# Moving row tiles in one transfer over 128 partitions, in a fused convolution and feed-forward kernel

## The chip, the cores and the metric

The kernel runs on one core of one Trainium2 chip. The metric is the device time of one execution in microseconds. A core has TensorE (PE, matrix products), VectorE (DVE), ScalarE (ACT), GpSimd (POOL) and SyncE (SP). Transfers between memory (HBM) and the on-chip SBUF, whose tiles have up to 128 partitions, are issued from the queues of SP, ACT and POOL and carried out by 16 DMA engines.

## What is computed

All arrays are float32, S = 2048 rows of D = 576 columns. `A_q` is `x`; the hidden width of the feed-forward part is 4608.

```python
xn = layernorm(x)                                  # x = A_q, over the columns
# A: short causal convolution of k (4 taps, per column), times v,
kv = causal_conv4(k, shift_k) * v
# then a causal convolution over all 2048 rows by FFT, per column
y = irfft(rfft(pad(kv)) * rfft(pad(ssm_k)))[:S] + kv * ssm_D
# B: feed-forward
ffn = relu(xn @ w1) @ w2                           # w1 576 x 4608, w2 4608 x 576
out = x + xn * y + ffn
```

## The kernel before

**Rows.** The 2048 rows are split as row = 32p + 16u + t, with p in 0..63, u in 0..1 and t in 0..15. Tile t holds 128 rows of 576 columns: partitions 0 to 63 are the 64 rows of u = 0, partitions 64 to 127 those of u = 1. In memory the 64 rows of one u lie 32 rows apart, and the two series lie 16 rows from each other. The views `x`, `k`, `v`, `out` have the shape (u, p, t, d). `halves(u)` gives the partitions of one half, and `move` loads or stores a tile, or a pair of tiles t and t + 1, in two transfers, one for each half. Its argument `queues` names the queue of each.

**The feed-forward part** sets most of TensorE's work. It takes the hidden units in 36 visits over 18 pairs of 256 (`NPAIR`), in two halves of the rows; each block has four tiles (512 rows). A product in float32 is made of three products of operands that are rounded into a high and a low part (`split_into`, `relu`). `load_w1(n)` loads the first weights of a visit: 4 x 128 rows in one transfer, and the remaining 64 rows (576 = 4 x 128 + 64) twice, once into partitions 0 to 63 and once into 64 to 127. `load_w2` loads the second weights into `r`; `split_w2` turns them into `w`, which the `pso` matmuls read. `mm1` makes the `psh` matmuls.

**The row tiles of x** come in pairs: `load_acc` into the `acc` tiles, where the sums are kept as well, `later_xT` into `rows` for the second half, and `load_rest` into `xt` for the last step. Finished sums of the first eight tiles go to memory as `fin` and come back as `ft`.

**The convolution** is a stream (`conv`) whose steps are inserted between the matmuls of the feed-forward part by a count of work (`tick`). It has four parts: the transform of the filter (`fk`, tiles `zk`), that of kv (`fx`: `load` fetches a tile of k and one of v two tiles ahead of their use, results go to `zx`), the products and second transforms (`fm`, results to `zy`), and the way back (`fo`: loads `zo`, `xt`, and `ft`; stores eight tiles of the output from `y` on POOL's queue). The other eight tiles of the output are stored from `acc` at the very end; the very last tile goes in column halves, each in two transfers, one on SP's queue and one on ACT's.

**Order.** The program is written in the order of the feed-forward visits; a scheduler then orders each engine's instructions. Each engine and each queue takes its instructions strictly in that order.

Of the kernel before, what the change touches and what calls it, by code (L numbers as in the profile page):

```python
# [17 lines left out]
P = 128  # L18
# [13 lines left out]
BT = T // NB  # L32
# [5 lines left out]
U = S // (T * A1)  # L38
# [71 lines left out]
def h3_ffn_kernel(ctx: ExitStack, tc, x, k, v, shift_k, ssm_k, ssm_D, w1, w2, fwd, inv, mid, out):  # L110
    nc = tc.nc
    x = x[0].rearrange("(p u t) d -> u p t d", u=U, t=T)
    k = k[0].rearrange("(p u t) d -> u p t d", u=U, t=T)
    v = v[0].rearrange("(p u t) d -> u p t d", u=U, t=T)
    out = out[0].rearrange("(p u t) d -> u p t d", u=U, t=T)
# [31 lines left out]
    acc = {}  # L147

    def place(b):

        return 1 - b if b < HB else b - HB

    def halves(u):

        return slice(u * A1, (u + 1) * A1), slice((1 - u) * A1, (2 - u) * A1)

    def move(tile_, rows, t, store=False, queues=(nc.sync, nc.sync)):
        for u in range(U):
            a, b = tile_[halves(u)[0]], rows[u, :, t]
            queues[u].dma_start(*((b, a) if store else (a, b)))  # L160

    pairs = {}

    def load_x(t, tag, bufs, late=False, **queues):
        pair = xp.tile([P, 2, D], F32, tag=tag, name=f"acc{t}", bufs=bufs)
        if late:
            with here():
                nc.vector.memset(pair[:, :, :1], 0.0)
        move(pair, x, slice(t, t + 2), **queues)
        return pair  # L170

    def load_acc(t, **queues):
        pairs[t] = load_x(t, f"acc{place(t // BT)}", BT // 2, **queues)
        acc[t], acc[t + 1] = pairs[t][:, 0, :], pairs[t][:, 1, :]

    def stats(t, src):
# [26 lines left out]
    done = {}  # L203
# [100 lines left out]
    def later_xT(b):  # L304
# [16 lines left out]
        for i in range(0, BT, 2):  # L321
            with here():
                if b == HB:
                    nc.vector.memset(hold[:, i * D:i * D + 1], 0.0)
                move(hold[:, i * D:(i + 2) * D].rearrange("p (t d) -> p t d", t=2), x,
                     slice(b * BT + i, b * BT + i + 2))
# [110 lines left out]
    def load_w1(n):  # L437
        f0 = (n % NPAIR) * FC
        r1 = both_w1[:, 5:] if n < NPAIR and n % 2 else both_w1
        for o, step in ((0, P), (P, FC - P)) if n == 0 else ((0, FC),):  # L440
            f, to = slice(f0 + o, f0 + o + step), slice(o, o + step)
            queue = nc.gpsimd if n == 0 and o == 0 else nc.sync
            queue.dma_start(r1[:, :4, to], w1[:4 * P, f].rearrange("(c p) f -> p c f", p=P))
            for h in range(2):
                queue.dma_start(r1[64 * h:64 * h + 64, 4, to], w1[4 * P:, f])
        raw_w[n] = r1
        weights[n] = {}

# [166 lines left out]
    def unit(ns, s, b, i, h, last):  # L615

        t = b * BT + i
        cols = slice(i * P, (i + 1) * P)
        final = b >= HB and last
        if final:  # L620
            while t not in added:
                next(stream)
        ps = ps_o.tile([P, 512], F32, tag="o", name=f"pso{ns[0]}_{t}_{h}")
        dc = slice(h * NH, (h + 1) * NH)
        seq = []
        for n in ns:
            for j in range(FT):
                hh, ll = hid[n, s, j]
                w = weights[n]["w2", h][:, :, j]
                seq += [(hh[:, cols], w[:, 0]), (hh[:, cols], w[:, 1]), (ll[:, cols], w[:, 0])]  # L630
        for c, (a, m) in enumerate(seq):
            done["pe"] = nc.tensor.matmul(ps[:, :NH], a, m, start=c == 0,  # L632
                                          stop=c == len(seq) - 1)
            if c % 6 == 5:
                tick(6 * NH)
        if b == 0:
            done["acc"] = nc.vector.scalar_tensor_tensor(
                acc[t][:, dc], ps[:, :NH], rstd[:, t:t + 1], acc[t][:, dc],
                op0=OP.mult, op1=OP.add)
        else:  # L640
            done["acc"] = nc.vector.tensor_tensor(acc[t][:, dc], ps[:, :NH], acc[t][:, dc],  # L641
                                                  OP.add)
        if final and t == T - 1:
            for u, queue in ((0, nc.sync), (1, nc.scalar)):
                queue.dma_start(out[u, :, t, dc], acc[t][halves(u)[0], dc])
        elif last and h:
            if t < HT:
                if t % 2:
                    nc.sync.dma_start(fin[t // 2], pairs[t - 1])
            elif t == T - 2:  # L650
                move(acc[t], out, t, store=True)
            elif t % 2:
                move(pairs[t - 1], out, slice(t - 1, t + 1), store=True)
# [7 lines left out]
    def fill():  # L661
        room = 2
        while work and work[0][0] <= room:
            size, args = work.pop(0)
            unit(*args)
            room -= size
# [23 lines left out]
    @contextmanager  # L690
    def here():


        with tc.issue_after(done["acc"].ins), tc.issue_after(done["act"].ins):
            yield

    def conv():
# [5 lines left out]
        with hold_pool as kp:  # L703
# [3 lines left out]
            win, gates, sums, uses = {}, {}, {}, [0]  # L707

            def slot(i):
                return both[:, i * D:(i + 1) * D]  # L710
# [7 lines left out]
            def load(t):  # L718
                win[t] = slot(WIN + t % (KS + 1))
                if t >= 0:  # L720
                    move(win[t], k, t, queues=(nc.sync, nc.sync))
                    gates[t] = slot(GATE + t % 2)
                    move(gates[t], v, t, queues=(nc.sync, nc.sync))
                else:
                    nc.gpsimd.memset(win[t][0:1, :], 0.0)
                    nc.sync.dma_start(win[t][1:A1, :], k[1, 0:A1 - 1, T + t, :])
                    nc.sync.dma_start(win[t][A1:, :], k[0, :, T + t, :])

            def first_loads():
                with here():  # L730
                    for j, t in enumerate((0, *range(-1, -KS, -1), 1)):
                        if j < KS:
                            nc.sync.dma_start(sk[:, j, :], shift_k[j:j + 1, :].to_broadcast([P, D]))
                        load(t)

            with tc.tile_pool(name="fk", bufs=2) as fp:
# [3 lines left out]
                for b in range(0, NH // Q, KB):  # L740
                    with here():
                        nc.vector.memset(kr[:, b:b + KB, :1], 0.0)
                    for q in range(4):
                        h, r = divmod(q, 2)
# [35 lines left out]
                for n, t2 in enumerate(order):  # L780
                    stk, nxt = nxt, []
                    u, t = divmod(t2, T)
# [94 lines left out]
        with tc.tile_pool(name="fm", bufs=2) as fp:  # L877
# [22 lines left out]
            def run(hi, lo, d, h):  # L900
# [7 lines left out]
                return ps[:, :NH], cols  # L908

            load(zk, 0, "k")  # L910
            load(zx, 0, "x")
            yield -PAUSE
# [69 lines left out]
        with tc.tile_pool(name="fo", bufs=2) as fp:  # L982
# [37 lines left out]
            def add(i):  # L1020
                if i >= 0:
                    t = order[i]
                    to, more = (ys[i], sums[i]) if t < HT else (acc[t], acc[t])
                    with here():
                        nc.vector.scalar_tensor_tensor(to, ys[i], rstd[:, t:t + 1], more,
                                                       op0=OP.mult, op1=OP.add)
                    if t < HT:
                        move(to, out, t, store=True, queues=(nc.gpsimd, nc.gpsimd))
                    else:
                        added.add(t)  # L1030

# [5 lines left out]
            for n, (t, u) in enumerate(units):  # L1037
# [7 lines left out]
                for h in range(2):  # L1045
# [20 lines left out]
                    yield W_FO  # L1066
            gate(T - 1)
            add(T - 1)


# [9 lines left out]
    def tick(cost):  # L1080

        if clock["done"] or clock["ffn"] < clock["until"]:
            clock["ffn"] += cost
            return
        clock["ffn"] += cost
        clock["conv"] += rate * cost
        if clock["conv"] < 0:
            return
        try:
            c = next(stream)  # L1090
        except StopIteration:
            clock["done"] = True
            return
        if c < 0:
            clock["conv"] = min(clock["conv"], 0.0)
            clock["until"] = clock["ffn"] - c
        else:
            clock["conv"] -= c

    warm = xp.tile([P, 512], mybir.dt.bfloat16, tag="m5", name="warm", bufs=1)  # L1100
    nc.vector.memset(warm, 0.0)
    for t in range(0, BT, 2):
        load_acc(t, queues=(nc.sync, nc.scalar))
    load_w1(0)
    table = const.tile([P, 1], F32, name="table")
    nc.vector.memset(table, 1.0)
# [12 lines left out]
    with tc.issue_after(done["act"].ins):  # L1119
        split_rest(0, 1)  # L1120
    load_w1(1)
    for t in range(BT, HT, 2):
        load_acc(t)
# [57 lines left out]
    for q, (n, s) in enumerate(visits):  # L1181
        half, m = divmod(n, NPAIR)
        b = HB + s if half else 1 - s
# [70 lines left out]
```

## Time and profile before

| | |
|---|---|
| median of 3 runs | 1058.05 us (1057.59 to 1059.14) |
| profiled execution | 1057.93 us, of which the span of the instructions is 1056.2 us |
| granted TensorE clock | 1.0 |
| busy: PE, DVE, ACT, POOL | 1047.1, 743.9, 550.7, 398.2 us |
| moved by DMA | 204.45 MB, mean 194 GB/s |

The profile is one execution. An engine's busy time counts its instructions of work; transfers are issued by instructions of a queue (SPq, ACTq, POOLq) and carried out by the DMA engines, whose share is a mean over all 16. The chain of waits goes back from the last instruction: at each step to what released it.

### The profile page before, as it was taken

How to read it: one execution, taken by the hardware profiler on the slowest of the kernel's cores; microseconds unless marked ns; L12 is line 12 of the kernel's file. 1: busy time of each engine (PE TensorE's matmuls, PEld its weight loads, DVE VectorE, ACT ScalarE, POOL GpSimd, SP SyncE). 2: the span in 40 equal slices, each digit the busy share in tenths (PEclk: the TensorE clock that was granted, in tenths of full speed). 3: DMA queues.
4: the chain of work that ended last, by engine and by line, in shares of the span. 5: the costliest groups of instructions: out<-in, count | busy, mean ns of one | idle time of the engine just before them, and what ended most of it. 6: DMA issues, size and time to landing. Idle time of an engine off the chain costs nothing.

```text
span 1056.2 us, 20042 instructions
## 1 busy us (share of the span) xinstructions
PE 1047.1 (99%) x7153; PEld 988.2 (94%) x7153; DVE 743.9 (70%) x1316; ACT 550.7 (52%) x1201; POOL 398.2 (38%) x398
## 2 busy tenths in 40 slices
PE   8999999999999999999999999999999999999998
PEld 5889999999999999999999999999999999999997
DVE  5539778787776788773477887778877773666664
ACT  5226566534343444433277787687777773444341
POOL 4133333333222333352443534343433444544641
PEclk9999999999999999999999999999999999999999
DMA  9944867777566766755876655656555648776864
GB/s 230 205 98 134 226 172 209 201 227 212 151 191 178 212 177 197 239 164 187 277 219 193 192 173 166 195 172 197 167 177 175 183 127 264 221 228 214 287 191 113
DMA packets 156304, 204.45 MB, mean 194 GB/s; under 512 B 32846, under 2 KB 122704, under 8 KB 155181
## 3 DMA queue, kind: packets, MB, share of 16 engines
q1 hardware_dynamic: 143308, 189.00, 60.5%
q0 software_dynamic: 12576, 13.44, 5.6%
q8 instruction: 56, 0.92, 0.4%
q10 hardware_dynamic: 320, 0.74, 0.3%
q14 instruction: 44, 0.35, 0.1%
HBM read 133.92 MB, written 55.05 MB: 179 GB/s over the span
## 4 chain that ended last, share of the span: by engine, by line
PE 97%; DVE 1%; DMA 1%; ACT 0%; issue 0%; SPq 0%; DVEq 0%
PE pso L632 43%; PE psh L569 22%; PE psb L545 14%; PE psf L907 7%; PE psa L545 6%; PE psf L687 3%; PE psf L1051 1%; PE psf L1053 1%; DMA acc<-in_x 1%; DVE bn L179 0%; PE psf L278 0%; ACT hh L551 0%; DVE lok L897 0%; DVE acc L641 0%; DVE yl L932 0%
## 5 line engine op out<-in xcount | busy, mean ns | idle before, releaser
L632 PE MATMUL pso<-w,hh 128*128 128x288 f32 x2304 | 468.9, 295 | 1.6 <-ACT w L531 0.8
L632 PEld LDWEIGHTS pso<-w,hh 128*128 128x128 f32 x2304 | 372.5, 188 | 9.8 <-ACT w L531 1.2
L632 PE MATMUL pso<-w,ll 128*128 128x288 f32 x1152 | 329.5, 295 | 0.0
L431 POOL TENSOR_TENSOR g<-both_w,g 128x256 fp32r<-128x256 f32 (+2 forms) x145 | 168.4, 1167 | 374.1 <-ACT g L469 322.4
L569 PE MATMUL psh<-b,g 128*128 128x512 f32 x864 | 218.2, 395 | 0.5 <-ACT b L226 0.2
L632 PEld LDWEIGHTS pso<-w,ll 128*128 128x128 f32 x1152 | 213.3, 188 | 1.1
L569 PEld LDWEIGHTS psh<-b,g 128*128 128x128 f32 x864 | 156.9, 188 | 30.5 <-DVE b L227 0.5
L641 DVE TENSOR_TENSOR acc<-pso,acc 128x288 f32<-128x288 f32 x232 | 101.7, 450 | 61.9 <-PE pso L632 59.1
L431 POOL TENSOR_TENSOR w<-r,w 128x576 fp32r<-128x576 f32 x72 | 113.0, 1570 | 53.8 <-ACT w L531 53.7
L551 ACT ACTIVATE hh<-psh 128x512 fp32r<-128x512 f32 x72 | 42.9, 597 | 143.8 <-PE psh L569 143.8
L552 DVE SCALAR_TENSOR_TENSOR ll<-psh,hh 128x512 fp32r<-128x512 f32 x72 | 49.4, 687 | 69.8 <-ACT hh L551 69.3
L545 PE MATMUL psb<-t,g 128*128 128x256 f32 x648 | 94.9, 280 | 0.1
L545 PEld LDWEIGHTS psb<-t,g 128*128 128x128 f32 x648 | 85.5, 188 | 0.4 <-DVE psa L600 0.3
L469 ACT ACTIVATE g<-both_w 128x256 fp32r<-128x256 f32 (+2 forms) x145 | 76.3, 543 | 9.9 <-PE psb L545 6.6
L498 POOL TENSOR_TENSOR both_w<-both_w 128x256 f32<-128x256 f32 x72 | 62.8, 891 | 30.3 <-DMA both_w<-in_w 29.0
L545 PE MATMUL psa<-b,g 128*128 128x256 f32 x432 | 63.1, 280 | 0.0
L551 ACT ACTIVATE hh<-psa 128x512 fp32r<-128x512 f32 x36 | 21.5, 598 | 72.9 <-PE psa L545 72.7
L545 PE MATMUL psb<-b,g 128*128 128x256 f32 x432 | 57.5, 281 | 0.0
L545 PEld LDWEIGHTS psa<-b,g 128*128 128x128 f32 x432 | 56.6, 188 | 0.0
L545 PEld LDWEIGHTS psb<-b,g 128*128 128x128 f32 x432 | 54.4, 188 | 0.2
L950 DVE TENSOR_TENSOR k<-psf,k 128x288 f32<-128x288 f32 x64 | 29.0, 454 | 35.1 <-ACT sw L949 33.3
L673 POOL DMA_DIRECT2D wx<-in_fwd x32 | 17.6, 551 | 95.3 <-PE psf L687 85.6
(135 smaller groups left out, 1695.3 us busy)
## 6 DMA issues: line engine op xcount, KB each, us to landing
r<-in_w SPq DMA_DIRECT2D x72, 288.0 KB, 4.0
zy<-vo SPq DMA_DIRECT2D x64, 288.0 KB, 2.9
zo<-zy SPq DMA_DIRECT2D x32, 576.0 KB, 4.4
both_w<-in_w SPq DMA_DIRECT2D x35, 512.0 KB, 4.2
zk<-zk SPq DMA_DIRECT2D x64, 144.0 KB, 2.6
ztk<-zk SPq DMA_DIRECT2D x32, 288.0 KB, 3.4
ztx<-zx SPq DMA_DIRECT2D x32, 288.0 KB, 3.5
k<-k SPq DMA_DIRECT2D x64, 144.0 KB, 3.3
```

Of the source, the lines that this page charges most:

```text
L431: return nc.gpsimd.tensor_tensor(dst, src, hi, OP.subtract)
L469: nc.scalar.activation(hi, src, AF.Copy)
L498: nc.gpsimd.tensor_tensor(dst, a, b, op)
L545: done["pe"] = nc.tensor.matmul(ps, a, m, start=start and i == 0, stop=i == len(seq) - 1, skip_group_check=not start)
L551: done["act"] = nc.scalar.activation(hh, ps, AF.Relu)
L552: lows.append(nc.vector.scalar_tensor_tensor(ll, ps, 0.0, hh, op0=OP.max, op1=OP.subtract))
L569: done["pe"] = nc.tensor.matmul(ps, a, m, start=i == 0, stop=i == len(seq) - 1)
L632: done["pe"] = nc.tensor.matmul(ps[:, :NH], a, m, start=c == 0, stop=c == len(seq) - 1)
L641: done["acc"] = nc.vector.tensor_tensor(acc[t][:, dc], ps[:, :NH], acc[t][:, dc], OP.add)
L687: nc.tensor.matmul(ps[:, :NH], w[:, n, :], stk, start=n == 0, stop=n == 1)
L907: nc.tensor.matmul(ps[:, :NH], a, m[:, cols], start=n == 0, stop=n == 2)
L950: nc.vector.tensor_tensor(k1[:, cols], ps, k1[:, cols], OP.mult)
```

## The change

Every transfer of a row tile, or pair of tiles, is made once over 128 partitions, where there were two over 64. The view in memory then has two series of 64 rows as its outer dimensions, (u, p, d); the tile in SBUF has 128 partitions. The same is done for the 64 remaining rows of the first weights: one transfer whose source is the 64 rows, repeated twice by a step of 0. Of the first two pairs of x, the one on SP's queue and the other on ACT's are now whole pairs, where both queues had half of each. The last tile's two column halves go one on SP's queue and one on ACT's. The number of transfers goes from 904 to 793.

```diff
-    def move(tile_, rows, t, store=False, queues=(nc.sync, nc.sync)):
-        for u in range(U):
-            a, b = tile_[halves(u)[0]], rows[u, :, t]
-            queues[u].dma_start(*((b, a) if store else (a, b)))
+    def move(tile_, rows, t, store=False, queue=nc.sync):
+        a, b = tile_, rows[:, :, t]
+        done["move"] = queue.dma_start(*((b, a) if store else (a, b)))
...
-            for h in range(2):
-                queue.dma_start(r1[64 * h:64 * h + 64, 4, to], w1[4 * P:, f])
+            queue.dma_start(r1[:, 4, to], w1[4 * P:, f][None].to_broadcast([2, 64, step]))
...
         if final and t == T - 1:
-            for u, queue in ((0, nc.sync), (1, nc.scalar)):
-                queue.dma_start(out[u, :, t, dc], acc[t][halves(u)[0], dc])
+            (nc.scalar if h else nc.sync).dma_start(out[:, :, t, dc], acc[t][:, dc])
...
-                    move(win[t], k, t, queues=(nc.sync, nc.sync))
+                    move(win[t], k, t)
...
-                        move(to, out, t, store=True, queues=(nc.gpsimd, nc.gpsimd))
+                        move(to, out, t, store=True, queue=nc.gpsimd)
...
-    for t in range(0, BT, 2):
-        load_acc(t, queues=(nc.sync, nc.scalar))
+    for t, queue in ((0, nc.sync), (2, nc.scalar)):
+        load_acc(t, queue=queue)
```

The order of the instructions stays nearly the same on all engines. SP's queue at the start, before; a row is a line, an instruction, its tiles and the partitions and sizes that it writes:

```order
L160 DMA acc_97<-in_x 64x1152
L160 DMA acc_100<-in_x 64x1152
L443 DMA both_w_94<-in_w 128x4x128
L445 DMA both_w_94<-in_w 64x128 x2
L443 DMA both_w_94<-in_w 128x4x256
L445 DMA both_w_94<-in_w 64x256 x2
L160 DMA acc_229<-in_x 64x1152 x2
L160 DMA acc_232<-in_x 64x1152 x2
L452 DMA r_0_0_235<-in_w 128x2x288
```

The same place after the change, down to the first load of second weights (`r`):

```order
L159 DMA acc_97<-in_x 128x1x1152
L442 DMA both_w_94<-in_w 128x4x128
L443 DMA both_w_94<-in_w 128x1x128
L442 DMA both_w_94<-in_w 128x4x256
L443 DMA both_w_94<-in_w 128x1x256
L159 DMA acc_224<-in_x 128x1x1152
L159 DMA acc_226<-in_x 128x1x1152
L450 DMA r_0_0_228<-in_w 128x2x288
```

Pairs of equal rows became one, nothing passed anything else, and the second pair of x went to ACT's queue altogether. SP's queue at the end, the eight tiles of the output that are stored from `acc`, before:

```order
L160 DMA out<-acc_6146 64x1152 x2
L160 DMA out<-acc_6200 64x1152 x2
L160 DMA out<-acc_5879 64x1152 x2
L160 DMA out<-acc_5927 64x576 x2
L645 DMA out<-acc_5927 64x288 x2
```

And after the change, where the row shows memory's side with its two series of 64:

```order
L159 DMA out<-acc_6082 2x64x1152
L159 DMA out<-acc_6135 2x64x1152
L159 DMA out<-acc_5818 2x64x1152
L159 DMA out<-acc_5865 2x64x576
L642 DMA out<-acc_5865 2x64x288
```

Here too each pair of transfers became one in the same place; of the last tile SP stores one column half in 128 rows, where it stored 64 rows of both.

More of the change, by code (lines that the diff above doesn't have):

```diff
@@ L155, in halves, with load_x @@
         return slice(u * A1, (u + 1) * A1), slice((1 - u) * A1, (2 - u) * A1)
-    def move(tile_, rows, t, store=False, queues=(nc.sync, nc.sync)):
-        for u in range(U):
-            a, b = tile_[halves(u)[0]], rows[u, :, t]
-            queues[u].dma_start(*((b, a) if store else (a, b)))
+    def move(tile_, rows, t, store=False, queue=nc.sync):
+        a, b = tile_, rows[:, :, t]
+        done["move"] = queue.dma_start(*((b, a) if store else (a, b)))
     pairs = {}
-    def load_x(t, tag, bufs, late=False, **queues):
+    def load_x(t, tag, bufs, late=False, **queue):
         pair = xp.tile([P, 2, D], F32, tag=tag, name=f"acc{t}", bufs=bufs)
@@ L168, in load_x, with load_acc @@
                 nc.vector.memset(pair[:, :, :1], 0.0)
-        move(pair, x, slice(t, t + 2), **queues)
+        move(pair, x, slice(t, t + 2), **queue)
         return pair
-    def load_acc(t, **queues):
-        pairs[t] = load_x(t, f"acc{place(t // BT)}", BT // 2, **queues)
+    def load_acc(t, **queue):
+        pairs[t] = load_x(t, f"acc{place(t // BT)}", BT // 2, **queue)
         acc[t], acc[t + 1] = pairs[t][:, 0, :], pairs[t][:, 1, :]
@@ L720, in load @@
                 if t >= 0:
-                    move(win[t], k, t, queues=(nc.sync, nc.sync))
+                    move(win[t], k, t)
                     gates[t] = slot(GATE + t % 2)
-                    move(gates[t], v, t, queues=(nc.sync, nc.sync))
+                    move(gates[t], v, t)
                 else:
```

## Prediction

> **What bounds the kernel now.** I read the page first (span, engines, DMA), then the chain of waits, then the list of DMA issues, and last a table of stages. From the page:
>
> ```profile
> span 1056.2 us, 20042 instructions
> PE 1047.1 (99%) x7153; PEld 988.2 (94%) x7153; DVE 743.9 (70%) x1316; ACT 550.7 (52%) x1201; POOL 398.2 (38%) x398
> DMA  9944867777566766755876655656555648776864
> DMA packets 156304, 204.45 MB, mean 194 GB/s; under 512 B 32846, under 2 KB 122704, under 8 KB 155181
> q1 hardware_dynamic: 143308, 189.00, 60.5%
> q0 software_dynamic: 12576, 13.44, 5.6%
> ...
> PE 97%; DVE 1%; DMA 1%; ACT 0%; issue 0%; SPq 0%; DVEq 0%
> ```
>
> TensorE is busy for 99% of the span and carries 97% of the chain; a transfer is on the chain only at the start. A shorter transfer can therefore win next to nothing after the start. A much longer one can still lose, if it outgrows the room that the DMA engines have: they are some 66% full (60.5% and 5.6% for the two large queues). The DMA line shows the same in 40 slices: full at the start, six to eight tenths later. So the question is what the one transfer over 128 partitions does to the sixteen DMA engines.
>
> **How a transfer is dealt over the DMA engines.** The list of DMA issues has the groups that move (first nine lines; of `both<-in_k`, 32 of the 35) and three that tell how dealing works (last three); columns are count, size of one, and median us from issue to landing.
>
> ```profile
> both<-in_k SPq DMA_DIRECT2D x35, 144.0 KB, 4.5
> both<-in_v SPq DMA_DIRECT2D x32, 144.0 KB, 3.2
> xt<-in_x SPq DMA_DIRECT2D x32, 144.0 KB, 3.8
> both_w<-in_w SPq DMA_DIRECT2D x70, 64.0 KB, 4.0
> acc<-in_x SPq DMA_DIRECT2D x14, 288.0 KB, 5.2
> rows<-in_x SPq DMA_DIRECT2D x8, 288.0 KB, 4.3
> out<-y POOLq DMA_DIRECT2D x16, 144.0 KB, 4.5
> out<-acc SPq DMA_DIRECT2D x6, 288.0 KB, 3.5
> acc<-in_x ACTq DMA_DIRECT2D x2, 288.0 KB, 6.0
> rows<-nrm SPq DMA_DIRECT2D x36, 64.0 KB, 2.7
> both<-in_k SPq DMA_DIRECT2D x3, 141.8 KB
> skip<-in_ssm_D SPq DMA_DIRECT2D x2, 1.1 KB
> ```
>
> ACT's own queue shows the rule plainly. In the last 6.2 us it issues two transfers of 64 rows, and its queue has 160 packets: 2 x 64 rows, and 32 more, 16 for each transfer.
>
> ```profile
> q10 hardware_dynamic: 160, 0.15, 8.0%
> out<-acc ACTq DMA_DIRECT2D x2, 72.0 KB
> ```
>
> So a transfer ends in one small packet on each engine that it ran on. Over the whole page 32846 packets are under 512 B. The 36 `rows<-nrm` transfers move 64 KB in runs of 128 B, 512 packets each, 18432 in all; 14414 are left. The groups of the list add up to 904 transfers, and 16 each would be 14464. Fifty are missing. The list has three transfers of 63 rows (141.8 KB is 63 x 2304 B) and two of a single row. If 63 rows are dealt over 9 engines and one row over 1, the shortage is 3 x 7 + 2 x 15 = 51, which is right but for one stray packet. Nine is the largest number up to 16 that divides 63. A transfer is thus dealt in equal shares of its rows, and where the rows cannot be cut into sixteen, it uses fewer engines.
>
> The changed transfer has 128 partitions in SBUF, but in memory its rows are two series of 64 (row p of half u lies at 32p + 16u + t, so the two halves cannot be written as one series). The outermost count is 2 on that side. No row of the trace has such a pattern, so its price lies between two cases: 2 engines, if the outermost series is what is cut, and 16, if the 128 rows are. The nearest row is that of 63 rows, which sixteen engines could have shared unevenly and did not; both sides must be cut alike, and two is the only cut that both outermost counts allow. I take 2 and keep 16 as a rival.
>
> The Trainium skill, DMA: Bandwidth & Descriptors, section "Why a DMA increments its semaphore by 16 and not by 1", says that the engine count is the largest number up to 16 that divides the slowest dimension of both access patterns, and its section "Rules for kernel authors" warns of an outermost dimension below 16. By that the count here is 2 and the sum is the one below; the 63-row transfers agree (9), and no run here shows a two-sided case yet.
>
> **The price of one MB.** A table of stages, from the trace by windows (length, busy time of five engines with counts, granted clock, DMA share, GB/s):
>
> ```profile
> 0.00:65.00 65.00, 60.95 (x329) 48.59 (x330) 29.30 (x79) 21.53 (x43) 18.40 (x23) 1.00 0.79 187
> 65.00:198.00 133.00, 133.00 (x806) 121.27 (x805) 103.38 (x193) 75.18 (x171) 47.41 (x56) 1.00 0.66 177
> 198.00:449.00 251.00, 251.00 (x1509) 228.23 (x1508) 194.50 (x310) 101.31 (x202) 77.14 (x77) 1.00 0.70 201
> 517.00:570.00 53.00, 53.00 (x408) 52.39 (x408) 37.61 (x69) 35.23 (x78) 22.31 (x20) 1.00 0.75 223
> 570.00:878.00 308.00, 307.91 (x2352) 303.83 (x2351) 238.37 (x417) 228.79 (x512) 124.58 (x108) 1.00 0.59 174
> 878.00:1041.00 163.00, 163.00 (x1252) 160.97 (x1251) 101.72 (x192) 65.51 (x151) 81.53 (x90) 1.00 0.73 226
> 879.00:881.00 2.00, 2.00 (x18) 2.00 (x17) 0.69 (x2) 0.65 (x3) 1.44 (x3) 1.00 1.00 399
> ```
>
> The last row is a moment with all sixteen engines full: 399 GB/s, 24.9 GB/s for one. A moved MB puts 1/16 of itself on each engine now and 1/2 on two engines then: on those two it adds 7/16 MB at 24.9 GB/s, 17.6 us. Present work of an engine is its share times the stage's length. Averaged over the page an engine gives 18.5 GB/s while busy (189.00 MB in 60.5% of 16 x 1056.2 us), so beside fourteen idle neighbours the old work may shrink to 18.5/24.9 = 0.74 of that; this is the low end of each term. A row tile is 2 x 144.0 KB = 0.295 MB, the remaining weight rows of one visit 2 x 64.0 KB = 0.131 MB.
>
> **The change by parts.** All transfers of one queue stand in order on each engine, so whatever is behind a moved one on those two engines (weights, the transforms' loads and stores) lands late too, its other fourteen shares notwithstanding. The first and last issues place the groups:
>
> ```profile
> L160 SPq DMA_DIRECT2D acc<-in_x x14: 465/596/1272, 0.8 to 542.7; - x14
> L160 SPq DMA_DIRECT2D rows<-in_x x8: 465/553/1227, 65.1 to 250.8; - x8
> L160 SPq DMA_DIRECT2D both<-in_k x32: 465/587/648, 198.7 to 445.9; - x32
> L160 SPq DMA_DIRECT2D xt<-in_x x32: 465/580/1324, 878.2 to 1009.5; - x32
> L160 POOL DMA_DIRECT2D out<-y x16: 527/543/559, 979.7 to 1038.5; - x16
> L160 SPq DMA_DIRECT2D out<-acc x8: 466/556/974, 1041.3 to 1050.7; - x8
> ```
>
> *The start.* The chain now:
>
> ```profile
> 1.41 8.39 DMA acc<-in_x
> 20.71 0.58 ACT w L531
> 21.33 0.66 PE pso L632 x3
> ```
>
> Eight row tiles (2.36 MB) and the remaining weight rows of visits 0 and 1 (0.26 MB) stand ahead of the first second-layer weights `r` on SP's queue. On two engines they take 2.62 / 2 / 24.9 = 52.6 us, and the 128-row weight loads between them some 2; so `r` lands near 56 instead of before 20.7, and TensorE, which needs it for `pso`, starts that 35 us late. If only the first two pairs held it, 1.18 MB would land at 1.4 + 23.7 = 25.1 instead of 9.8: 15 us. The stage's balance (0.79 x 65 = 51.4, plus 3.02 MB x 17.6 = 53.1, against 65) gives 39. I take 35, from 15 to 39. That tiles 2 and 3 now come wholly by ACT's queue costs nothing: nothing stands behind them there before the last stores.
>
> *65 to 198.* Four row tiles and four visits' rests, 1.70 MB: 87.8 + 30 = 118 us in 133. The room covers it: 0. Without cover one block of 1.18 MB holds everything behind it for 23.7 us, the high end.
>
> *198 to 449, the loads of k and v.* 32 tiles, four of `rows`, nine rests: 11.8 MB, 207 us. With 0.70 x 251 = 175.7 that is 383 us of work in 251: +132; with the old work shrunk to 130, +86. TensorE's order is fixed, the transforms of these tiles stand between its other matmuls, and tiles are loaded only two ahead, so it waits. I take 105, nearer the low end, because the fourteen neighbours do stand idle.
>
> *517 to 570.* Eight row tiles, two rests, 2.62 MB: 39.8 + 46 = 86 in 53, +33. The next 308 us are 59% full (182, and 21 for nine rests), so much can be made up: 0 to 33, I take 15. That next stage itself stays covered.
>
> *878 to 1041.* Sixteen x tiles and five rests, 5.38 MB, 95 us, and eight `out<-y` tiles, 2.36 MB, 41 us, on POOL's queue. Old work 119. With all of it on the same two engines: 255 in 163, +92; with y elsewhere and old work shrunk to 88: +20. I take 45.
>
> *The end.* Eight tiles of `out<-acc`, the last cut in two, are issued from 1041.3: 2.36 MB / 2 / 24.9 = 47.4 us, so they end near 1088.7 instead of 1056.2: +32.
>
> *Saved.* 111 of 904 issues, about 0.58 us of SP each. SP waits for others at most issues, so I count 0; up to 0.6 us of it is on the chain at the start.
>
> Sum: 35 + 0 + 105 + 15 + 45 + 32 = 232 us. The profiled execution took 1057.93 us (span 1056.2 and 1.7 around it), 0.1 under the median of 1058.05. 1057.9 + 232 gives **1290 us**. The low ends add up to 15 + 86 + 20 + 32 = 153 (1211 us), the high ends to 39 + 24 + 132 + 33 + 92 + 32 = 352 (1410 us).
>
> **Rivals.**
> 1. *Sixteen engines, no difference.* If the 128 rows are cut, the same bytes run at the same rate, TensorE's 97% of the chain is untouched, and only the issues go: 1057 to 1059, say 1057.9. For it: nothing in the trace denies it directly. Against it: the 63 rows. The Trainium skill, same page, "Rules for kernel authors", advises one 128-partition transfer in place of two over halves, since the halves share the engines anyway; no run here shows that yet. Chance 0.06.
> 2. *Two engines, but hidden in the middle.* If waits ahead of use are long enough, only start and end pay: 1057.9 + 35 + 32 = 1125. Against it: 383 us of work in 251 is no matter of lateness. It needs old work of 44 us in that stage, not 130. Chance 0.07.
> 3. *Faster, through the start.* If whole pairs ran better on sixteen engines than halves do, the first two pairs (1.18 MB) could land after 3.0 us at 399 GB/s in place of 8.39, at most 5.4 us less: 1052.5. It decides from 2.1 us saved. Against it: the DMA line shows the engines at nine tenths in that slice already, so other transfers share the time. Chance 0.04.
>
> **How the numbers follow.** Two engines that become the bound: 0.83, of which 0.03 beyond 1410 from waits that the balance leaves out. The range goes from a little under the sum of low ends, 1180, to 1410; what lies outside is rivals 1 to 3 and that tail, 0.20. Runs of before lie within 0.15%, so 0.2% is what can be told from no change. Slower: 0.83 + 0.07 = 0.90; the same 0.06; faster 0.04.
>
> **What would show it.** Packets under 512 B: 222 transfers of 16 go and 111 of 2 come, so about 29,500 (1776 fewer, 31,070, if sixteen engines share them). ACT's queue: 260 packets for its two transfers of 128 rows, not 288. Landing of `both<-in_k` over 6 us even alone, of `acc<-in_x` over 20. `r` near 56 us. TensorE under 85% busy, with idle slices from 198 to 449 and after 878 that end in DMAs, while the mean DMA share falls. I am wrong if these counts show 16; and if they show 2 with TensorE busy from 198 to 449, the balance is wrong.

## The result, and the profile after

The changed kernel takes 1334.47 us (median; 1332.43 to 1339.22) against 1058.05 us: 1.2617 times as long, with a 95% interval from 1.2592 to 1.2642. That is 276 us more. The prediction was 1290 us, from 1180 to 1410. From the page of the changed kernel:

```profile
span 1331.4 us, 19885 instructions
PE 1096.8 (82%) x7152; PEld 1026.8 (77%) x7153; DVE 743.1 (56%) x1316; ACT 551.0 (41%) x1201; POOL 392.3 (29%) x389
PE   2499899968478887877987699999999997988770
...
DMA  2383566544244455553663456666666456556611
...
DMA packets 156777, 204.45 MB, mean 154 GB/s; under 512 B 33337, under 2 KB 123195, under 8 KB 155656
q1 hardware_dynamic: 140308, 188.99, 46.5%
q0 software_dynamic: 16112, 13.47, 4.5%
...
q10 hardware_dynamic: 260, 0.74, 0.2%
...
PE 59%; DMA 24%; SPq 7%; issue 3%; DVE 1%; POOL 1%; ACT 1%; POOLq 0%; ACTq 0%; DVEq 0%
```

The same 204.45 MB move, and the DMA engines are less busy on average (46.5% and 4.5%, where they had 60.5% and 5.6%), yet DMA now carries 24% of the chain, where it had 1%. The mean hides two full engines among fourteen with time on their hands. The counts show how the moved transfers are dealt. ACT's queue has 260 packets: its two transfers of 128 rows, and two small packets each. SP's queue has 3000 packets fewer than before: its 200 moved transfers of 16 small packets became 100 of two.

The table of stages (length; busy PE, PEld, DVE, ACT, POOL; granted clock, DMA share, GB/s), cut where the groups of transfers begin (600 to 677.9 us is left out):

```profile
0.00:107.50 107.50, 65.39 (x328) 51.97 (x330) 29.93 (x79) 21.61 (x43) 18.14 (x22) 0.81 0.44 113
107.50:249.30 141.80, 136.24 (x809) 123.86 (x808) 104.05 (x192) 75.20 (x171) 47.89 (x57) 0.98 0.59 168
249.30:600.00 350.70, 268.50 (x1505) 241.01 (x1504) 193.55 (x308) 100.96 (x202) 76.55 (x76) 0.88 0.47 142
677.90:749.10 71.20, 47.49 (x314) 45.35 (x313) 26.09 (x52) 24.60 (x53) 15.91 (x15) 0.88 0.42 133
749.10:1071.90 322.80, 322.76 (x2453) 318.65 (x2454) 250.90 (x437) 240.13 (x537) 129.12 (x111) 1.00 0.60 175
1071.90:1278.60 206.70, 177.69 (x1262) 172.98 (x1261) 101.44 (x193) 65.71 (x151) 78.32 (x84) 0.93 0.57 177
1278.60:1331.40 52.80, 9.95 (x74) 9.62 (x73) 5.08 (x11) 0.60 (x1) 0.00 (x0) 0.62 0.13 50
```

The last row is the plainest: TensorE ends in its first ten us or so, then nothing but the output's stores runs. The share of sixteen engines is 0.13, about 2/16, and they move 50 GB/s, 25 GB/s each. From 1290 to 1300 us stores of SP's and of ACT's queue are under way (packets, MB, share of sixteen engines):

```profile
q1 hardware_dynamic: 100, 0.45, 10.9%
q10 hardware_dynamic: 66, 0.08, 2.1%
```

Together that is still about two sixteenths, however many stores are waiting: the transfers of both queues share the same two engines. The fifth row is the other end: a stage with few moved transfers, in which TensorE is busy throughout.

The same kernel's five longest waits of TensorE in total (us in all, times, longest; in the kernel before, the longest of this list has 1.2 us in all), and pieces of its chain of waits (start, length, what), at the start, in the late loads of x and in the last part:

```profile
PE psf L684 <- DMA xs<-both: 80.2, 12, 28.5
PE psf L261 <- DVE xn L199: 22.2, 1, 22.2
PE pso L630 <- DVE acc L639: 18.9, 4, 7.6
PE pso L630 <- ACT w L529: 17.9, 1, 17.9
PE psf L1048 <- DMA zo<-zy: 14.4, 7, 3.5
```

```profile
33.58 27.31 DMA r<-in_w
...
687.03 21.81 DMA acc<-in_x
710.49 6.00 DMA both_w<-in_w
721.81 26.36 DMA acc<-in_x
...
1155.22 34.00 DMA zo<-zy x2
```

`xs`, `zo` and `r` were not moved. Before, they landed within a few us (the last number, a median):

```profile
xs<-both SPq DMA_DIRECT2D x32, 144.0 KB, 2.4
zo<-zy SPq DMA_DIRECT2D x32, 576.0 KB, 4.4
r<-in_w SPq DMA_DIRECT2D x72, 288.0 KB, 4.0
```

They still use all sixteen engines, since the moved transfers account for all of the 3000 packets that SP's queue lost. That two of their sixteen shares wait behind moved transfers is concluded: the trace does not name the engine of a packet. That is how a transfer which nobody needs yet stops TensorE: it delays the next one, which somebody needs.

By stages, each measured from the first issue of one group to that of the next (at 65.1, 198.7, 513.6, 553.8, 876.9 and 1041.3 us before, at 107.5, 249.3, 677.9, 749.1, 1071.9 and 1278.6 us after):

| from | before | after | forecast |
|---|---|---|---|
| start, to `rows<-in_x` | 65.1 | 107.5, +42.4 | +35 |
| to `both<-in_k` | 133.6 | 141.8, +8.2 | 0 |
| to `ztk<-zk` | 314.9 | 428.6, +113.7 | +105 |
| to `zy<-vo` | 40.1 | 71.2, +31.1 | +15 |
| to `zo<-zy` | 323.1 | 322.8, -0.3 | 0 |
| to `out<-acc` | 164.4 | 206.7, +42.3 | +45 |
| to the end | 14.9 | 52.8, +37.9 | +32 |

The differences add up to 275.3 us, the difference of the spans (1331.4 - 1056.2 = 275.2) but for rounding.

### The profile page after: what moved, and what is told of

It reads as the page before. It is cut to its first block, busy times and chain, and to the rows that moved or that the text cites. A ratio compares the mean times of both kernels' runs of the same rounds, so it can differ in the third digit from the quotient of the medians.

```text
span 1331.4 us, 19885 instructions
## 1 busy us (share of the span) xinstructions
PE 1096.8 (82%) x7152; PEld 1026.8 (77%) x7153; DVE 743.1 (56%) x1316; ACT 551.0 (41%) x1201; POOL 392.3 (29%) x389
## 2 busy tenths in 40 slices
DMA packets 156777, 204.45 MB, mean 154 GB/s; under 512 B 33337, under 2 KB 123195, under 8 KB 155656
## 3 DMA queue, kind: packets, MB, share of 16 engines
q1 hardware_dynamic: 140308, 188.99, 46.5%
q0 software_dynamic: 16112, 13.47, 4.5%
## 4 chain that ended last, share of the span: by engine, by line
PE 59%; DMA 24%; SPq 7%; issue 3%; DVE 1%; POOL 1%; ACT 1%; POOLq 0%; ACTq 0%; DVEq 0%
PE pso L630 26%; PE psh L567 13%; PE psb L543 8%; DMA zo<-zy 6%; PE psf L904 5%; DMA xs<-both 5%; PE psa L543 4%; DMA acc<-in_x 4%; PE psf L684 2%; DMA r<-in_w 2%; DMA zk<-zk 2%; SPq L864 2%; SPq L443 1%; DMA both_w<-in_w 1%; SPq L442 1%
## 5 line engine op out<-in xcount | busy, mean ns | idle before, releaser
L630 PE MATMUL pso<-w,hh 128*128 128x288 f32 x2304 | 487.9, 304 | 39.0 <-DVE acc L639 18.9
L630 PEld LDWEIGHTS pso<-w,hh 128*128 128x128 f32 x2304 | 388.8, 196 | 49.1 <-DVE acc L639 20.3
L630 PE MATMUL pso<-w,ll 128*128 128x288 f32 x1152 | 338.4, 302 | 0.0
L567 PE MATMUL psh<-b,g 128*128 128x512 f32 x864 | 225.8, 406 | 0.1
L630 PEld LDWEIGHTS pso<-w,ll 128*128 128x128 f32 x1152 | 221.9, 195 | 1.1
L684 PE MATMUL psf<-xs,wx 128*128 128x288 f32 x128 | 30.5, 322 | 80.2 <-DMA xs<-both 80.2
L684 PEld LDWEIGHTS psf<-xs,wx 128*128 128x128 f32 x128 | 23.1, 201 | 85.9 <-issue 54.9
L685 ACT ACTIVATE both<-psf 128x288 f32<-128x288 f32 x43 | 17.5, 408 | 105.8 <-DMA zx<-both 60.9
L529 ACT ACTIVATE w<-r 128x576 fp32r<-128x576 f32 x72 | 48.6, 674 | 25.7 <-DMA r<-in_w 25.7
L635 DVE SCALAR_TENSOR_TENSOR acc<-pso,rstd,acc 128x288 f32<-128x288 f32 x72 | 36.5, 510 | 38.6 <-PE pso L630 38.1
```

Source lines behind the costliest of these rows:

```text
L529: nc.scalar.activation(t[:, 0], r2, AF.Copy)
L567: done["pe"] = nc.tensor.matmul(ps, a, m, start=i == 0, stop=i == len(seq) - 1)
L684: nc.tensor.matmul(ps[:, :NH], w[:, n, :], stk, start=n == 0, stop=n == 1)
```

## The experiments

The theory before these runs: a transfer whose rows lie in memory as two series runs on two DMA engines, and these two, always the same ones on SP's queue, become the bound of the full stages. The rivals: the larger single transfer is slow whatever its pattern; or each late transfer costs its own delay, and no throughput is at stake. Times are medians, ratios against the kernel before on the same chip (1058.17 to 1058.44 us).

| kernel | us | ratio, 95% interval |
|---|---|---|
| `one_series` | 1055.45 | 0.9971 (0.9960 to 0.9982) |
| `four_series` | 1134.17 | 1.0717 (1.0686 to 1.0748) |
| `kv_one` | 1130.54 | 1.0680 (1.0658 to 1.0701) |
| `k_one` | 1079.79 | 1.0200 (1.0168 to 1.0233) |
| `kv_pool` | 1071.39 | 1.0122 (1.0092 to 1.0151) |
| `start_one` | 1095.39 | 1.0349 (1.0318 to 1.0379) |
| `rows_one` | 1073.94 | 1.0148 (1.0118 to 1.0177) |
| `acc_late_one` | 1089.76 | 1.0295 (1.0265 to 1.0325) |
| `xt_one` | 1099.04 | 1.0383 (1.0353 to 1.0413) |
| `y_one` | 1059.45 | 1.0010 (0.9999 to 1.0021) |
| `end_one` | 1092.49 | 1.0320 (1.0300 to 1.0341) |
| `w1_one` | 1067.68 | 1.0089 (1.0059 to 1.0118) |

**One series of rows.** Against the changed kernel:

```diff
-    x = x[0].rearrange("(p u t) d -> u p t d", u=U, t=T)      # k, v, out alike
+    x, k, v, out = (a[0].rearrange("(q t) d -> q t d", t=T) for a in (x, k, v, out))
...
-        a, b = tile_, rows[:, :, t]
+        a, b = tile_, rows[:, t]
...
-            queue.dma_start(r1[:, 4, to], w1[4 * P:, f][None].to_broadcast([2, 64, step]))
+            queue.dma_start(r1[:, 4, to], w1[4 * P - 64:, f])
```

> The changed kernel with every moved transfer still one over 128 partitions, but with its rows in memory as a single series of 128 (row = 16q + t), and the remaining weight rows read as rows 448 to 575. The convolution therefore works on other rows than the reference's, and partitions 0 to 63 get other weight rows; sizes, counts and order are the changed kernel's. Two-engine theory (the outer series of 2 confines a transfer to two DMA engines, and these become the bound): all sixteen engines, 1052 to 1060 us, ACT's queue with 288 packets and SP's with 16 small packets for each transfer. Rival (the larger single transfers are what holds the queues, whatever their pattern): 1250 to 1335 us.

1055.45 us, 0.29% under the kernel before. The page:

```profile
span 1053.7 us, 19885 instructions
DMA packets 154509, 204.43 MB, mean 194 GB/s; under 512 B 31069, under 2 KB 120927, under 8 KB 153388
q10 hardware_dynamic: 288, 0.74, 0.2%
```

The number of instructions is the changed kernel's, 19885, and so are the 111 merged transfers and their sizes. Only the pattern in memory differs, and with it the whole loss is gone: 288 packets on ACT's queue are 16 small ones for each transfer, and 31069 small packets are within one of the 31,070 that the prediction gave for sixteen engines. The size of the transfer is out as a cause. As a program for this problem it is no gain: the halves of a tile must lie in separate halves of the partitions, because `stack` splits them into high and low parts by halves.

**Four series of rows.** Against the changed kernel: the views are `"(q w t) d -> w q t d"` with w = 4, and the weight rows 32 rows repeated four times.

> The changed kernel with each moved transfer still one over 128 partitions, but with its rows in memory as four series of 32 (row = 64q + 16w + t), and the remaining weight rows as 32 rows repeated four times. The convolution and the first products therefore work on other rows than the reference's; sizes, counts and order are the changed kernel's. If the outer count is the count of engines: four, so ACT's queue has 264 packets, and a moved MB adds (1/4 - 1/16)/24.9 = 7.5 us instead of 17.6: start 9, loads of k and v 0 to 13, late pairs of x 6 to 14, last part 0 to 14, end 9; 24 to 59 us more, 1082 to 1117 us. Rival (any transfer of more than one series goes to two engines): about 1334 us.

```profile
DMA packets 154869, 204.44 MB, mean 181 GB/s; under 512 B 31429, under 2 KB 121287, under 8 KB 153748
...
q10 hardware_dynamic: 264, 0.74, 0.2%
```

264 is four small packets for each of two transfers: the outer count in memory is the count of engines, 2 for 2 and 4 for 4. The rival is out. The size of the loss was missed: 76 us where 24 to 59 were expected. The stages grew by 19.8 (start; 9 expected), 26.7 (k and v; 0 to 13), 8.2 (late pairs; 6 to 14), 6.6 (last part; 0 to 14) and 16.0 us (end; 9). At four engines the balance of work shows little excess or none. That most of what is lost is therefore waiting, which the balance does not price, is concluded and not tried.

**k and v, and k alone.** Against the kernel before, `move` makes one transfer where asked:

```diff
+        if one:
+            a, b = tile_, rows[:, :, t]
+            queues[0].dma_start(*((b, a) if store else (a, b)))
+            return
...
-                    move(win[t], k, t, queues=(nc.sync, nc.sync))
+                    move(win[t], k, t, one=True)
...
-                    move(gates[t], v, t, queues=(nc.sync, nc.sync))   # not in k_one
+                    move(gates[t], v, t, one=True)
```

> The kernel before, with the loads of k and v alone made in one transfer over two series of 64. Two-engine theory as a bound on throughput: 9.44 MB x 17.6 us = 166 us on two engines beside 176 of old work in 251 us, so 91 us more (45 if the old work shrinks), 1103 to 1150 us. Rival (each late transfer stalls what waits for it, by about its own longer landing, some 6 us, on 32 transfers): up to 190 us more, or nothing at all if the tiles come early enough.

> The kernel before, with the loads of k alone in one transfer. Throughput bound: 83 us on the two engines beside 130 to 176 of old work, 213 to 259 in 251 us: 0 to 8 us more, 1058 to 1066 us. Rival (a price for each late transfer): half of what the loads of k and v together cost.

Together 72 us more, in the middle of what the balance gave (45 to 91). k alone cost 21.4 us (the median of 1076.98 and 1082.60; the trace is of the first): less than half of that, and more than the 0 to 8 of the balance. The trace parts it. From the first load of k to the first store of `zx`, where all of the first tiles are due at once, `k_one` needs 14.8 us more and `kv_one` 22.8: a wait for the first tiles. From there to the last `zx` store `k_one` needs 3.7 us more and `kv_one` 48.6. Half of the transfers cost a thirteenth of the steady loss: this part is a bound that is crossed between the two, not a price for each transfer. TensorE's longest wait in `kv_one` is for what stands behind:

```profile
PE psf L691 <- DMA xs<-both: 42.9, 11, 7.8
```

**k and v on POOL's queue.** As `kv_one`, with `queues=(nc.gpsimd, nc.gpsimd)`.

> The loads of k and v in one transfer each as in the experiment that cost 72 us, but issued on POOL's queue. If a transfer of two series takes the same two DMA engines from any queue: again 45 to 90 us more, 1103 to 1150 us. If POOL's transfers take a pair of engines that changes from one to the next, the work spreads over all sixteen: 0 to 15 us more, 1058 to 1073 us, the rest being the longer landing and 32 issues of some 0.8 us on POOL.

13 us more instead of 72, within what a changing pair was to give. From its page and its list of issues:

```profile
DMA packets 168078, 204.56 MB, mean 191 GB/s; under 512 B 46669, under 2 KB 136527, under 8 KB 166956
...
q0 software_dynamic: 29472, 23.00, 9.0%
...
both<-in_k POOLq DMA_DIRECT2D x16, 288.0 KB, 10.2
both<-in_v POOLq DMA_DIRECT2D x16, 288.0 KB, 11.6
```

A tile still takes 10 to 12 us to land, so each is on few engines; but the work of 32 tiles no longer piles up on the same two. The trace does not name the engines, so that the pair changes is concluded from the time.

**The other groups, one at a time**, each against the kernel before.

`start_one`: the first four pairs of x, the first on SP's queue and the second on ACT's.

> The kernel before, with the first four pairs of x alone in one transfer each, the first on SP's queue and the second on ACT's. Two-engine theory with order on the queue: 2.36 MB stand ahead of the first second-layer weights on the two engines, 47.4 us, so these land near 52 instead of before 20.7 and TensorE starts on them 31 us late: 1086 to 1096 us. Rival (only the first two pairs hold TensorE, later weights pass): 15 us, 1073 us.

```profile
0.75 27.55 DMA acc<-in_x
29.49 26.43 DMA r<-in_w
```

1095.39 us, 37 more. Both waits stand on its chain: for the first pairs, and then for the weights behind the last two. The order on the queue decides, as forecast.

`acc_late_one`: `load_acc(t, late=True, one=True)`.

> The kernel before, with the four pairs of x for the second half of the rows alone (517 to 543 us) in one transfer each. Balance of work, made up in the emptier stage behind: 0 to 15 us more, 1058 to 1073 us. Rival (TensorE waits for these tiles themselves, since their sums are due at once, and no room behind can repay it): each of the four lands 11.8 us after the one before it, 30 to 45 us more, 1088 to 1103 us.

```profile
516.50 7.53 DMA fin<-acc
...
524.25 21.88 DMA acc<-in_x
547.77 5.87 DMA both_w<-in_w
558.21 26.13 DMA acc<-in_x
```

31.6 us more: the rival holds. The tiles can be loaded only once `fin` has been stored from the same buffers, and the sums into them are due at once. The stage behind has room for bytes, but TensorE's idle time cannot be made up there, since TensorE is full in it.

`xt_one`: `move(xt, x, t, one=True)`.

> The kernel before, with the sixteen x tiles of the last part alone in one transfer each. Throughput bound: 4.72 MB x 17.6 us = 83 us on two engines beside 88 to 119 of old work in 163 us: 8 to 39 us more, 1066 to 1097 us. Rival (hidden, since tiles are loaded two ahead): 1057 to 1060 us.

40.9 us more, a little over the high end of the bound. `end_one`: the last eight tiles, from `acc`.

> The kernel before, with the eight tiles that are stored at the very end from acc alone in one transfer each. Two-engine theory: 2.36 MB at 2 x 24.9 GB/s from 1041.3 us on, 47.4 us, 32 to 38 us more, 1090 to 1096 us, with a DMA share of 2/16 = 0.13 over the last 40 us. Rival (sixteen engines): 1057 to 1059 us.

```profile
1051.00:1090.80 39.80, 0.67 (x6) 0.44 (x4) 0.83 (x2) 0.00 (x0) 0.00 (x0) 0.57 0.12 50
```

34 us more, all after TensorE has ended; two engines' share and 50 GB/s, as in the changed kernel.

`rows_one`: the pairs of x for the later blocks.

> The kernel before, with the four pairs of x for the later blocks (from 65 us and from 247 us on) alone in one transfer each. Balance of work: both stages have room for 1.18 MB more by half, 0 us, 1057 to 1060 us. Rival (a block of 23.7 us on the two engines holds what is queued behind it, the stores of the transforms above all, whatever room follows): 5 to 20 us for each of the two blocks, 1068 to 1098 us.

15.6 us more, so the rival of this one holds: 5.4 us after the first block and 10.8 us in the stage of k and v. After the first block its chain has

```profile
76.85 18.66 DMA r<-in_w
```

again the second weights, queued behind 23.7 us of x. `y_one`: the stores from `y` on POOL's queue.

> The kernel before, with the eight tiles stored from y on POOL's queue alone in one transfer each. If POOL's pair of engines changes from one transfer to the next, as the loads of k and v on POOL suggest: 1057 to 1063 us. If it is the same pair for all: 41 us more of work in the last 62 us before 1041, 10 to 25 us more.

1.2 us more, with an interval that holds 1: no difference that can be measured. `w1_one`: the remaining rows of the first weights.

> The kernel before, with the 64 remaining rows of the first weights alone in one transfer. Balance of work: 0.131 MB a visit, 2.3 us of it more on the two engines in stages that have room: only the start pays, 0.26 MB in the first two visits, 3 to 6 us; 1058 to 1065 us. Rival (each of 36 late landings is felt): 36 x 2.6 us, up to 1150 us.

9.4 us more, a little over the 1058 to 1065 that the balance gave; 7.2 of it come at the start. In the stage of k and v, where nine of these transfers run, it is 1.0 us.

The eight groups, each alone, add up to 242 us of the 276.

## Why the prediction was right

**Two engines.** The count of a leading 2 was taken from transfers of 63 rows on nine engines and of one row on one. `four_series` and `one_series` change only the pattern in memory, to outer counts of 4 and 128, and show four engines and sixteen: the outer count in memory decides. The Trainium skill's rule in DMA: Bandwidth & Descriptors, "Why a DMA increments its semaphore by 16 and not by 1", agrees with all three counts (2, 4, 16); its advice of one 128-partition transfer for two halves, in "Rules for kernel authors", holds in these runs only where the halves form one series, and the changed kernel is 26% slower by following it where they do not.

**The start**, +42.4 for +35: right in kind, and 3 us above the term's high end. The second weights landed at 60.9 (33.58 + 27.31) where 56 was forecast. `start_one` gives 38.2 us of the stage and `w1_one` 7.2.

**65 to 198**, +8.2 for 0: the step that failed is the cover. The stage has room for the bytes, as computed; but a block of 23.7 us on two engines holds the weights behind it, and `rows_one` shows 5.4 us of that alone.

**k and v**, +113.7 for +105: right, though in two parts that the working did not separate, a wait for the first tiles and a bound behind it. Alone, k and v give 71.7, `rows` 10.8 and the weight rows 1.0 us of that stage, 83 in all. Some 30 us appear only together. A full stage would explain that: nine weight rests, 1.18 MB x 17.6 us = 21 us of work, cost 1.0 us alone and would be paid in full once the two engines have no room. That they are the larger part of the 30 us was not tried.

**The late pairs**, +31.1 for +15: mis-sized. The high end of the term, 33, was right; the step that failed is "much can be made up". `acc_late_one` shows 30.0 us in this stage and nothing given back in the next.

**878 to 1041**, +42.3 for +45: right in size by luck, since two errors cancel. The x tiles alone cost 41.5, a little over the 39 that the balance gives for them when the old work does not shrink (83 + 119 - 163), and the stores from `y`, which had a part in the 45, cost nothing that can be measured.

**The end**, +37.9 for +32: right in kind, two engines at 50 GB/s; the stage took 52.8 us, where the stores were to take 47.4.

**Small packets**: 33,337 and not 29,500. SP's and ACT's fell as forecast; POOL's queue grew from 12576 packets to 16112 instead (last section).

The sum was 43 us short, by the two covers (8 and 16), k and v (9), the start (7) and the end (6), less 3 in the last part. Beside the waits TensorE itself became slower: the same matmuls took 1096.8 us instead of 1047.1, because the granted clock falls while it waits:

```profile
350.00:360.00 10.00, 0.00 (x0) 0.00 (x0) 0.75 (x2) 1.31 (x3) 0.00 (x0) 0.50 0.21 75
500.00:510.00 10.00, 3.08 (x13) 3.11 (x14) 2.09 (x3) 2.86 (x6) 0.00 (x0) 0.50 0.49 148
```

In both windows of the changed kernel it is 0.50, in the second with matmuls running: the `pso` matmuls of `w` with `hh` take 420 ns in the mean, where they took 295 before. The Trainium skill, TensorE: Matmul & The Clock Gate, "Part 1: The HAM clock gate", states that an idle window halves the clock until TensorE has been busy again; this trace agrees, and the prediction left it out. How much of the 276 us it is cannot be read off, since in a stage bound by DMA a slower TensorE costs nothing.

## What to carry to other kernels

Before merging transfers look at the outermost count of the pattern on both sides (these runs varied memory's side): on SP's and ACT's queues it, and not the size of the transfer, set how many of the sixteen DMA engines worked, and the count of small packets in the profile shows it. Price such a change by the work it puts on the busiest engine, stage by stage, and not by the mean DMA share; where that work exceeded the stage, the kernel paid about the excess. Where it does not, look for what is queued behind the slow transfer and is due soon: room later does not repay an engine that is full.

## What the runs showed beyond that

**An issue can stand still.** SP's queue at the start of the changed kernel (start, time that the issuing instructions took):

```profile
0.76 0.72 SPq L159 DMA_DIRECT2D acc<-in_x  x1
1.53 0.67 SPq L442 DMA_DIRECT2D both_w<-in_w  x1
2.25 14.12 SPq L443 DMA_DIRECT2D both_w<-in_w  x1
16.42 10.28 SPq L442 DMA_DIRECT2D both_w<-in_w  x1
```

The third and fourth issue, of one transfer each, took 14.12 and 10.28 us; the longest issue on SP's queue took 2.1 us in the kernel before and 1.6 us in `one_series`, whose transfers have the same sizes on sixteen engines. Over the whole execution SP's issues took 737 us instead of 398. Ahead of them stand, on each of two engines, 64 rows of the first pair on SP's queue and as many of the second on ACT's; it seems that SP cannot hand over more rows until some have gone. While it stands, nothing behind it on SP's queue reaches the fourteen idle engines either, and the chain gives SPq 7%, where it had 0. The last issue of `end_one`, behind the other stores, is another:

```profile
1065.90 11.98 SPq L648 DMA_DIRECT2D out<-acc  x1
```

**POOL's queue pads.** Each of the 32 tiles that `kv_pool` put on POOL's queue brought (29472 - 12576) / 32 = 528 packets. Against `kv_one`, whose small packets number 31885, there are (46669 - 31885) / 32 = 462 more under 512 B for each tile; with the two that a tile has there, 464. Sixteen of them are the ones that end a transfer. The other 448 carry next to nothing: the page has 0.11 MB more than that of `kv_one` (204.45 MB), about 8 bytes for each of them. 448 is 14 x 32, as if each of the fourteen engines without a share had one such packet for each of the 32 packets of rows on a working engine (528 - 464 = 64 of them, on two). `four_series` bears this reading out. With four engines it gives 64 + 16 + 12 x 16 = 272 packets for a tile, where two transfers of 64 rows made 64 + 32 = 96, so 8 x 176 = 1408 more for the eight stores from `y`; POOL's queue has 14000 packets there, 1424 more than before, with one transfer of weight rows among them.
